# Recurrence stage of a fused attention and mixture-of-experts kernel: two DVE scan operands move from SBUF to PSUM, and the loop's idle matrix products are taken out

## The chip, the cores and the metric

The kernel runs on one core of a Trainium2 chip. The metric is device microseconds (us) of one execution, as the median of several runs. The engines are named as the profile names them: PE multiplies matrices (PEld is its weight load), DVE, ACT and POOL are the vector, scalar and GpSimd engines, SP issues most DMAs. SBUF is the on-chip memory that all of them read; PSUM is the smaller memory into which PE writes its products, in banks of 2 KB per partition (512 f32).

## The reference, cut to what matters

```python
def _attn_ref(r, k, v, w, u):           # B, H, S, D = 2, 8, 768, 48
    state = zeros((B, H, D, D))
    for t in range(S):
        cur = einsum('bhd,bhe->bhde', u * k[t], v[t])
        y[:, :, t] = einsum('bhd,bhde->bhe', r[t], state + cur)
        state = w[t][..., None] * state + einsum('bhd,bhe->bhde', k[t], v[t])
    return y
x = y.transpose(0, 2, 1, 3).reshape(1536, 384)
x = _moe_ref(x)      # one of 8 experts per token: relu(x @ w1[e]) @ w2[e], times its gate weight
return (silu(x @ w_gate) * (x @ w_val)) @ w_out
```

## The kernel before

**Stages.** The recurrence is worked in 12 units of 128 tokens, six for each batch entry (about the first 80 us). A routing tail (to about 97 us) places every token's row in its expert's slots. Then come the eight experts (psh, pso) and the last layer (psg, psu), in which PE has one product behind the other. All work is written out in program order; each engine takes its own instructions in that order, and semaphores hold it where it needs another's result.

**A unit of the recurrence.** Decays are made into running products inside a unit of 2 x 64 tokens. For a unit u, DVE does this, in order:

- `prep1` (L369): two scans X, one for each half, over the decays `dm` (SBUF) with a constant operand `xinit` (SBUF), which is tiny but for a 1 at the place where a head's run starts.
- `xrow` (L533): x = y + aV for the unit before; y is in PSUM, aV in SBUF.
- `state` (L516, L519): d, the decay over a whole unit (4 elements, both operands in SBUF), then Sc = psP * d, the state carried on. PE's product psP stands in the same function, ahead of d.
- `anchored` (L377): the reciprocal of every eighth X into `anch`, in SBUF, one of two buffers.
- `prep2` (L415, L421, L424, L434): two scans R over `wm` (SBUF) and `anch` (SBUF), then M (two multiplies) and rk.

In the loop over u, DVE makes X, R and M for unit u + 2 while PE forms `scores` (psA, from M) for unit u + 1 and `values` (y) for unit u. ACT copies psA out of PSUM, and POOL masks the copy (`affine_select`, L472, reads and writes SBUF) and then makes aV for the next x (`own`, L449, reads SBUF).

**Order of PE in an iteration.** psP of `state(u)`, three idle products (`warm`, psW, 512 columns each, results unused), scores(u + 1), transposes for kgt, the rows psx, the transposes of x, values(u), and one small product `columns` into the tile lg, which holds the gate's logits and a column group a8 that ACT copies out for `own`.

**The names in the prediction.** X, x, d, Sc, R, M, rk, aV, psA, psP, psW, psx, y and lg are tiles as above; `wm` is made by ACT (`prep0`). PSUM tiles with one tag of a pool share a buffer in turn. The lines are those of the kernel before:

Of the kernel before, what the change touches and what calls it, by code (L numbers as in the profile page):

```python
# [24 lines left out]
C = 128  # L25
# [4 lines left out]
G = 8  # L30
# [12 lines left out]
def build(tc, cap, dm, tk, vt, ub, cst, wg, w1, w2, wgate, wval, wout, out):  # L43
# [237 lines left out]
    at = ExitStack()  # L281
    gp = at.enter_context(tc.tile_pool(name="gp", bufs=2))
    ac = at.enter_context(tc.tile_pool(name="ac", bufs=1))
    xinit = ac.tile([128, 2, NP, XW], F32, name="xinit")
    csb = ac.tile([128, 3 * E], F32, name="csb")
    ev, ebase, eend = (csb[:, E * i:E * i + E] for i in range(3))
    ud = ac.tile([128, NP, 32], F32, name="ud")
    fold = ac.tile([128, 32], F32, name="fold")
    wgs = ac.tile([128, 3, 32], F32, name="wgs")
    tri = ac.tile([128, 128], BF16, name="tri")  # L290
    ones = ac.tile([128, 128], BF16, name="ones")
# [6 lines left out]
    early = ExitStack()  # L298
    ep = early.enter_context(tc.tile_pool(name="ep", bufs=2, side="right"))
    dmt = [ep.tile([128, DMW], F32, name=f"dm{i}", bufs=1) for i in range(3)]  # L300
    anch = [ep.tile([128, 2 * (NP * HC + G - 1)], F32, name=f"anch{i}", bufs=1) for i in range(2)]
    wm = [ep.tile([128, 2, NP, HC], F32, name=f"wm{i}", bufs=1) for i in range(2)]
    Sb = [ac.tile([128, NP, 2 * D], F32, name=f"Sb{i}") for i in range(2)]
    ap2 = at.enter_context(tc.tile_pool(name="ap2", bufs=2))
# [1 line left out]
    psA = at.enter_context(tc.tile_pool(name="psA", bufs=1, space=PSUM))  # L306
    ps1 = at.enter_context(tc.tile_pool(name="ps1", bufs=1, space=PSUM))
    psY = at.enter_context(tc.tile_pool(name="psY", bufs=2, space=PSUM))

    vts, Xf, Xt, Mt, kgt, Sc, At, yt, xt, xgt, xgs, av, rkt, a8s, lgt = ({} for _ in range(15))  # L310

    def run(x, up):

        x = x.rearrange("p a b -> p (a b)")
        return x if up else x[:, ::-1]

    def anchors(x, h, o):

        return x[:, h, :, h * o:h * o + HC - G + 1:G]

    def halved(x, w):
        return x[:, 0:2 * NP * w].rearrange("p (h a j) -> p h a j", h=2, a=NP)
# [37 lines left out]
    def prep1(u):  # L360


        if u >= NU:
            return
        W = dmt[u % 3][:, 0:2 * NP * XW].rearrange("p (h a j) -> p h a j", h=2, a=NP)
        Xf[u] = ap3.tile([128, 2 * (NP * XW + G + 1)], F32, tag="X", name="X")
        X = Xt[u] = halved(Xf[u], XW)
        for h in range(2):
            nc.vector.tensor_tensor_scan(out=run(X[:, h], h), data0=run(W[:, h], h), data1=run(xinit[:, h], h),  # L369
                                         initial=0.0, op0=ALU.mult, op1=ALU.max)  # L370
            tick()

    def anchored(u):

        if u >= NU:
            return
        nc.vector.reciprocal(out=each8(anch[u % 2], HC), in_=each8(Xf[u], XW))  # L377
        tick()

    def check(u):  # L380

        if u >= NU:
            return
        for i, t in enumerate((each8(Xf[u], XW), each8(anch[u % 2], HC))):
# [24 lines left out]
    def prep2(u):  # L409

        if u >= NU:
            return
        Rt = ep.tile([128, 2, NP, HC], F32, tag="R", name="R")
        for h in range(2):
            nc.vector.tensor_tensor_scan(out=run(Rt[:, h], 1 - h), data0=run(wm[u % 2][:, h], 1 - h),  # L415
                                         data1=run(halved(anch[u % 2], HC)[:, h], 1 - h),
                                         initial=0.0, op0=ALU.mult, op1=ALU.add)
            tick()
        M = Mt[u] = ap3.tile([128, NP, 4, HC], F32, tag="M", name="M")
        kr = dmt[u % 3][:, 2 * NP * XW:].rearrange("p (a s j) -> p a s j", a=NP, s=4)  # L420
# [32 lines left out]
    def warm(n, ps=None, tag="T"):  # L453

        ps = (ps or psA).tile([128, 512], F32, tag=tag if ps else "A0", name="psW")
        x = xinit.rearrange("p h a j -> p (h a j)").bitcast(BF16)[:, 0:512]
        for _ in range(n):
            nc.tensor.matmul(ps, ones, x, start=True, stop=True)

    def scores(u):  # L460
        if u >= NU:
# [22 lines left out]
    def values(u, ps=range(NP)):  # L484

        if not ps[0]:
            yt[u] = psY.tile([128, DM], F32, tag="y", name="y")
        y, A = yt[u], At[u]
# [12 lines left out]

    def state(u):

        if not (u + 1) % UPB:
            return
        P = ps1.tile([128, NP, D], F32, tag="P", name="psP")
        k = kgt.pop(u)
        if u % UPB:
            nc.tensor.matmul(P, ident, Sc[u], start=True, stop=False, skip_group_check=True)
        for p in range(NP):  # L510
            for g in range(2):
                c0 = D * (2 * p + g)
# [16 lines left out]
    def xrow(u):  # L529
        if u < 0:  # L530
            return
        x = xt[u] = gp.tile([128, DM], F32, tag="x", name="x", bufs=7)
        nc.vector.tensor_tensor(out=x, in0=yt.pop(u), in1=av.pop(u), op=ALU.add)  # L533
        tick()

    gss = {}
# [64 lines left out]
    def choose(us, weigh=weigh):  # L601

        n = len(us)
        u0, u1 = us[0], us[-1] + 1
        lg = lgt[us][:, :, 0:E]

        def over(x):
            return x.to_broadcast([128, n, E])
# [38 lines left out]
    def count(us):  # L647

        u0, n = us[0] // 4 * 4, len(us)
        pc = lgt[us][:, :, 2 * E:]  # L650
        adds = [(ohacc, us[0])] * (u0 > 0) + [(ohs[:, q, :], max(us[0], q + 1)) for q in range(u0, us[-1])]
        nc.tensor.matmul(pc, tri, ohs[:, us[0]:us[-1] + 1, :], start=True, stop=False, skip_group_check=True)
# [204 lines left out]
    nc.vector.memset(xinit[:, 0, :, HC:HC + 1], 1.0)  # L857
    nc.vector.memset(xinit[:, 1, :, 1:2], 1.0)
    for i in range(2):
        nc.gpsimd.memset(wm[i], 0.0)  # L860
        nc.vector.memset(anch[i], 0.0)
    nc.vector.memset(ones, 1.0)
    prep0(0)
    prep1(0)
    anchored(0)
# [22 lines left out]
    for u in range(NU - 2):  # L888
        chosen, counted = ended.get(u - 2), ended.get(u - 3)
        if u:  # L890
            prep0(u + 2)
            prep1(u + 2)
        xrow(u - 1)
        state(u)
        anchored(u + 2)
        warm((7, 4)[u] if u < 2 else 3, ps1, "xT")
        scores(u + 1)
        if u:
            own(u)
# [3 lines left out]
        else:  # L903
# [6 lines left out]
            warm(2, ps1, "lg")  # L910
        expand(u)
        load_dm(u + 4)
        zero(NZ)
# [3 lines left out]
            ready += counted  # L917
        prep2(u + 2)
        if not u:
            check(1)  # L920
            nc.vector.tensor_copy(out=tri, in_=before)
        check(u + 2)
        if u:
            values(u)
            columns(u - 1, max(u - 2, 0), u + 1)
        else:
            values(u)
            for q in range(2):
                to = logits_to(q)
                nc.tensor.matmul(to[:, 0:E], gss.pop(q), fold[:, E:2 * E], start=True, stop=True)  # L930
            a8 = gp.tile([128, 2, H], F32, tag="a82", name="a82")
            nc.scalar.copy(out=a8, in_=lgt[group[0]][:, 0:2, 0:E])
            for q in range(2):
                a8s[q] = a8[:, q, :]
            own(0)
# [625 lines left out]
```

## Time and profile before

| | us |
|---|---|
| median of 3 runs | 465.55 (465.39 to 465.67) |
| the profiled execution, its own time | 465.57 |
| span of its trace, first to last instruction | 463.9 |
| recurrence loop, first X to the last rk | 3.76 to about 79.6 |
| experts' first product | 97.14 |

The profiled execution agrees with the median to 0.02 us; 1.67 us of its own time lie outside its span. A row of a timeline gives start and length in us, engine, line, operation, output <- inputs, shape and count, and in brackets what the engine sat idle for. [...]

### The profile page before, as it was taken

To read this page: it belongs to the slowest core of one execution; us is meant where nothing else is said; L and a number is where in the kernel's file an instruction comes from. 1 tells how busy PE (TensorE), PEld (TensorE's weight loads), DVE (VectorE), ACT (ScalarE), POOL (GpSimd) and SP (SyncE) were. 2 spreads that over 40 slices of the span, in tenths; PEclk is the share of its full clock that TensorE was granted. 3 is DMA by queue.
4 is the path that set the end of the run, shared out by engine and by line. 5 is a ranking of instruction groups with operands and counts; after the bars stand their busy time and mean duration, and the time that the engine had idled before them with its cause. 6 is when DMAs were issued, how large, how long until landed. Compare 5 with 4: busy or idle time off the path is not lost.

```text
span 463.9 us, 9305 instructions
## 1 busy us (share of the span) xinstructions
PE 450.2 (97%) x3565; PEld 397.8 (86%) x3576; DVE 331.0 (71%) x690; ACT 238.8 (51%) x561; POOL 70.9 (15%) x94
## 2 busy tenths in 40 slices
PE   7998999999999999999999999999999999999994
PEld 3676767889999999999988888888888888888884
DVE  8999999877887945858599876665678585434241
ACT  4556685666877866674446454544443352231120
POOL 3324355540000000000000650000000000003033
PEclk9999999999999999999999999999999999999999
DMA  7798994139999944336134455222200000001011
GB/s 247 219 290 266 314 279 163 70 103 305 378 350 361 357 171 144 91 116 199 42 101 131 75 68 70 68 68 69 68 1 0 3 0 0 1 0 69 0 70 68
DMA packets 34801, 62.57 MB, mean 135 GB/s; under 512 B 5504, under 2 KB 17280, under 8 KB 34752
## 3 DMA queue, kind: packets, MB, share of 16 engines
q1 hardware_dynamic: 32832, 57.20, 40.5%
q0 software_dynamic: 1920, 4.73, 2.8%
q8 instruction: 29, 0.48, 0.5%
q14 instruction: 20, 0.16, 0.1%
HBM read 52.48 MB, written 9.44 MB: 133 GB/s over the span
## 4 chain that ended last, share of the span: by engine, by line
PE 80%; DVE 9%; issue 4%; DMA 4%; ACT 1%; POOL 1%; POOLq 0%; SPq 0%; DVEq 0%; ACTq 0%
PE psg L1418 32%; PE psu L1441 14%; PE psh L1297 14%; PE pso L1315 13%; DMA dm<-in_dm 2%; DVE R L415 2%; DVE X L369 2%; DVE M L424 1%; POOL out L1453 1%; PE psA L469 1%; PE y L494 1%; PE y L499 1%; PE psx L1282 1%; DVE rk L434 1%; DVE anch L377 1%
## 5 line engine op out<-in xcount | busy, mean ns | idle before, releaser
L1418 PE MATMUL psg<-yb,wu 128*128 128x512 f32 x648 | 156.3, 395 | 0.0
L1418 PEld LDWEIGHTS psg<-yb,wu 128*128 128x128 f32 x648 | 121.3, 188 | 26.2
L1441 PE MATMUL psu<-wu,a 128*128 128x384 f32 x432 | 80.8, 336 | 0.0
L1441 PEld LDWEIGHTS psu<-wu,a 128*128 128x128 f32 x432 | 76.4, 188 | 2.9
L1297 PE MATMUL psh<-xe,wu 128*128 128x240 f32 x576 | 69.1, 277 | 0.9 <-DVE xe L835 0.9
L1297 PEld LDWEIGHTS psh<-xe,wu 128*128 128x128 f32 x576 | 66.2, 190 | 1.2 <-DVE xe L835 1.1
L1315 PE MATMUL pso<-h,wu 128*128 128x240 f32 x576 | 66.4, 275 | 0.0
L1315 PEld LDWEIGHTS pso<-h,wu 128*128 128x128 f32 x576 | 65.4, 189 | 0.0
L1425 DVE TENSOR_TENSOR t<-t,psg 128x512 f32<-128x512 f32 x36 | 24.7, 686 | 51.9 <-PE psg L1418 38.9
L213 DVE TENSOR_TENSOR wu<-raw,wu 128x512 fp32r<-128x512 f32 x96 | 61.6, 684 | 0.0
L207 ACT CAST wu<-raw 128x512 fp32r<-128x512 f32 x96 | 54.9, 620 | 3.0 <-PE pso L1315 1.4
L1430 ACT CAST a<-t 128x512 fp32r<-128x512 f32 x36 | 22.3, 620 | 60.3 <-DVE t L1425 60.3
L1304 DVE SCALAR_TENSOR_TENSOR h<-psh,h 128x240 fp32r<-128x240 f32 x64 | 25.0, 403 | 23.2 <-ACT h L1303 22.9
L207 ACT CAST wu<-bits 128x384 fp32r<-128x384 f32 x36 | 18.0, 513 | 42.0 <-DVE bits L200 41.9
L1453 POOL DMA_INDIRECT out<-acc,idc x12 | 11.7, 975 | 173.6 <-DVE acc L1451 172.1
L1330 POOL DMA_INDIRECT idl<-ids,dests x12 | 13.5, 1124 | 159.0 <-DVE dests L795 155.6
L1424 ACT ACTIVATE t<-psg 128x512 f32<-128x512 f32 x36 | 21.5, 597 | 30.2 <-PE psg L1418 30.1
L1431 DVE TENSOR_TENSOR a<-t,a 128x512 fp32r<-128x512 f32 x36 | 24.8, 689 | 13.2 <-ACT a L1430 13.2
L1303 ACT ACTIVATE h<-psh 128x240 fp32r<-128x240 f32 x64 | 23.3, 374 | 9.8 <-PE psh L1297 9.1
L1451 DVE TENSOR_TENSOR acc<-psu,acc 128x384 f32<-128x384 f32 x24 | 12.9, 558 | 19.9 <-PE psu L1441 19.9
L471 ACT COPY A<-psA 128x512 f32<-128x512 f32 x24 | 12.8, 586 | 19.0 <-PE psA L469 19.0
L472 POOL TENSOR_SCALAR_AFFINE_SELECT A<-A 128x512 f32<-128x512 f32 x24 | 15.4, 665 | 43.6 <-ACT A L471 43.6
(156 smaller groups left out, 554.5 us busy)
## 6 DMA issues: line engine op xcount, KB each, us to landing
raw<-in_moe_w SPq DMA_DIRECT2D x32, 768.0 KB, 10.8
scr<-zrow SPq DMA_DIRECT2D x12, 384.0 KB, 4.9
raw<-in_moe_w_gate SPq DMA_DIRECT2D x6, 768.0 KB, 4.8
raw<-in_moe_w_val SPq DMA_DIRECT2D x6, 768.0 KB, 4.4
raw<-in_moe_w_out SPq DMA_DIRECT2D x6, 768.0 KB, 4.3
dm<-in_dm SPq DMA_DIRECT2D x18, 192.0 KB, 4.4
v<-in_tk SPq DMA_DIRECT2D x12, 192.0 KB, 6.5
dm<-in_dm SPq DMA_DIRECT2D x18, 99.0 KB, 4.7
```

Of the source, the lines that this page charges most:

```text
L207: nc.scalar.copy(out=slot_t[u % NSLOT][:, 0, c:c + n], in_=bits[i])
L213: nc.vector.tensor_tensor(out=w[:, 1, c:c + n], in0=bits.pop(i), in1=R(w[:, 0, c:c + n]), op=ALU.subtract)
L1297: nc.tensor.matmul(ps, w[:, a, k, c0:c0 + 128], xet[e][:, b, k, :], start=n == 0, stop=n == 8)
L1303: nc.scalar.activation(out=h[:, 0, :], in_=ps, func=AF.Relu)
L1304: nc.vector.scalar_tensor_tensor(out=h[:, 1, :], in0=ps, scalar=0.0, in1=R(h[:, 0, :]), op0=ALU.max, op1=ALU.subtract)
L1315: nc.tensor.matmul(ypt[e, d], w[:, a, f % 4, 128 * d:128 * d + 128], h[:, b, :], start=f == 0 and n == 0, stop=f == 7 and n == 2)
L1418: nc.tensor.matmul(gps[i][g], w[:, a, g, k, c0:c0 + 128], yb[t, k][:, c], start=a_ == k == 0, stop=a_ == k == 2)
L1424: nc.scalar.activation(out=t, in_=pg[0], func=AF.Silu)
L1425: nc.vector.tensor_tensor(out=t, in0=t, in1=pg[1], op=ALU.mult)
L1430: nc.scalar.copy(out=a[:, 0], in_=t)
L1431: nc.vector.tensor_tensor(out=a[:, 1], in0=t, in1=R(a[:, 0]), op=ALU.subtract)
L1441: nc.tensor.matmul(out_ps[t, j], att[i][:, c, 128 * j:128 * j + 128], w[:, a, f % 4, :], start=f % FP == 0 and n == 0, stop=f % FP == FP - ...
```

## The change

- `anch` becomes one tile in PSUM (a whole bank, 512 f32), no longer two in SBUF. The reciprocal writes to it and the R scans and ACT's check read from it.
- `xinit` becomes one half's worth (264 f32) in PSUM. It lies in one bank, `tots`, with the state's product psP.
- Since PE writes to that bank and DVE's X scans read from it, `state(u)` (now only the product) is issued before `prep1(u + 2)`, and d and Sc move into `moved(u)` at the place where they stood.
- The small product `columns` goes into columns 384 on of the y tile (made 512 wide), and ACT copies both logits and a8 from there to an SBUF tile `lgs`. `choose` then reads the logits from SBUF for the first eight units.
- `warm` in the loop stays only in its first two turns (7 and 4 products); the eight iterations behind them, which had three each, have none. Its operands are now a tile `idle` of ones.
- ACT's `check(1)` is issued earlier, behind `prep2(1)`.

```diff
-    xinit = ac.tile([128, 2, NP, XW], F32, name="xinit")
-    anch = [ep.tile([128, 2 * (NP * HC + G - 1)], F32, name=f"anch{i}", bufs=1) for i in range(2)]
+    anch = ps1.tile([128, 2 * NP * HC], F32, tag="lg", name="anch")
+    tots = ps1.tile([128, NP * D + NP * XW], F32, tag="P", name="tots")
+    xinit = tots[:, NP * D:]
+    inv = anch.rearrange("p (h a j g) -> p h a j g", h=2, a=NP, g=G)[..., 0]
+    lgs = ac.tile([128, NU - 3, 2 * E], F32, name="lgs")
...
-            nc.vector.tensor_tensor_scan(out=run(X[:, h], h), data0=run(W[:, h], h), data1=run(xinit[:, h], h),
+            nc.vector.tensor_tensor_scan(out=run(X[:, h], h), data0=run(W[:, h], h), data1=xinit,
...
-        nc.vector.reciprocal(out=each8(anch[u % 2], HC), in_=each8(Xf[u], XW))
+        nc.vector.reciprocal(out=inv, in_=each8(Xf[u], XW))
...
-                                         data1=run(halved(anch[u % 2], HC)[:, h], 1 - h),
+                                         data1=turned(anch[:, h * (NP * HC - G + 1):][:, 0:NP * HC], 1 - h),
...
-        P = ps1.tile([128, NP, D], F32, tag="P", name="psP")
+        P = psp[u] = tots[:, 0:NP * D].rearrange("p (a d) -> p a d", a=NP)
...
+    def moved(u):
+
+        if u not in psp:
+            return
+        P = psp.pop(u)
         d = ap2.tile([128, NP], F32, tag="d", name="d")
...
         if u:
             prep0(u + 2)
+            state(u)
             prep1(u + 2)
         xrow(u - 1)
-        state(u)
+        moved(u)
         anchored(u + 2)
-        warm((7, 4)[u] if u < 2 else 3, ps1, "xT")
+        if u < 2:
+            warm((7, 4)[u], ps1, "xT")
         scores(u + 1)
```

On DVE, the order within an iteration stays as it was; what differs is what the scans read and what they wait for. The iteration in which DVE prepares unit 4, before (X_484 is its X, dm1 its decays, anch0 its anchors; the waits name the engine or DMA queue whose semaphore is awaited):

```order
L369 SCALAR_TENSOR_TENSOR X_484<-dm1_111,xinit_94 128x264 [waits DMAHW1_49,DMAHW0_49]
L369 SCALAR_TENSOR_TENSOR X_484<-dm1_111,xinit_94 128x264
L533 TENSOR_TENSOR x_487<-y_452,aV_413 128x384 [waits PE_49,Pool_49]
L516 TENSOR_TENSOR d_499<-X_256,X_373 128x4
L519 TENSOR_TENSOR Sc_501<-psP_489,d_499 128x192 [waits DVE_49,PE_49]
L377 RECIPROCAL anch0_113<-X_484 128x2x32
L415 SCALAR_TENSOR_TENSOR R_553<-wm0_115,anch0_113 128x256 [waits DVE_49,Activation_49]
L415 SCALAR_TENSOR_TENSOR R_553<-wm0_115,anch0_113 128x256 [waits Activation_49]
```

The same iteration in the changed kernel:

```order
L372 SCALAR_TENSOR_TENSOR X_487<-dm1_110,tots_132 128x264 [waits DMAHW1_49,DMAHW0_49,PE_49]
L372 SCALAR_TENSOR_TENSOR X_487<-dm1_110,tots_132 128x264
L543 TENSOR_TENSOR x_490<-y_447,aV_408 128x384 [waits Activation_49,Pool_49]
L526 TENSOR_TENSOR d_492<-X_266,X_378 128x4
L529 TENSOR_TENSOR Sc_494<-tots_132,d_492 128x192 [waits DVE_49]
L380 RECIPROCAL anch_131<-X_487 128x64
L418 SCALAR_TENSOR_TENSOR R_542<-wm0_112,anch_131 128x256 [waits DVE_49,Activation_49]
L418 SCALAR_TENSOR_TENSOR R_542<-wm0_112,anch_131 128x256 [waits Activation_49]
```

The wait for PE has moved from Sc up to the first X scan, and X and R now have one operand in PSUM (tots, anch); d still has both in SBUF.

On PE, the place between one unit's values and the next one's scores, before (psW is the idle product, psA the scores):

```order
L576 MATMUL lg_362<-fold_97,xT_543 128x16 [waits Activation_49]
L509 MATMUL psP_602<-Sc_501,ident_70 128x192 [waits DVE_49]
L513 MATMUL psP_602<-v_369,kgt_530 64x48 [waits DMAHW6_49]
L513 MATMUL psP_602<-v_369,kgt_530 64x48 x7
L458 LDWEIGHTS ones_100
L458 MATMUL psW_617<-xinit_94,ones_100 128x512 [waits PE_49]
L458 LDWEIGHTS ones_100
L458 MATMUL psW_617<-xinit_94,ones_100 128x512
L458 LDWEIGHTS ones_100
L458 MATMUL psW_617<-xinit_94,ones_100 128x512
L469 MATMUL psA_622<-M_556 128x128 [waits DVE_49]
```

The same place in the changed kernel:

```order
L588 MATMUL y_554<-fold_96,xT_532 128x16 [waits Activation_49]
L511 MATMUL tots_132<-Sc_494,ident_70 128x192 [waits DVE_49]
L515 MATMUL tots_132<-v_365,kgt_519 64x48 [waits DMAHW6_49]
L515 MATMUL tots_132<-v_365,kgt_519 64x48 x7
L471 MATMUL psA_605<-M_545 128x128 [waits DVE_49,PE_49]
```

The three idle products are gone, so the scores follow the state's product at once; the state's product keeps its place on PE.

## Rows read from the trace of the kernel before

**Rows 1.** Busy time by stretch: PE, PEld, DVE, ACT, POOL, then granted clock, DMA share, GB/s

```profile
79.40:86.70 7.30, 7.23 (x136) 6.37 (x138) 6.16 (x26) 4.99 (x13) 2.64 (x4) 1.00 0.01 2
20.00:60.00 40.00, 37.40 (x614) 28.68 (x620) 39.07 (x81) 26.00 (x76) 13.78 (x18) 1.00 0.95 293
60.00:80.00 20.00, 19.56 (x336) 15.32 (x338) 19.38 (x37) 13.13 (x45) 12.93 (x15) 1.00 0.75 231
```

**Rows 2.** Chain that ended last: start, length, engine, tile, line

```profile
61.40 0.48 DVE x L533
61.92 0.55 PE psx L547 x3
...
97.14 8.54 PE psh L1297 x72
```

**Rows 3.** DVE groups, 8 to 61.9 us (units 1 to 8): count, busy, mean ns

```profile
L415 DVE TENSOR_TENSOR_SCAN R<-wm,anch 128x256 f32<-128x256 f32 x16 | 14.2, 921 | 0.7
```

**Rows 4.** DVE groups, 3 to 8 us (unit 0, before POOL's first mask)

```profile
L415 DVE TENSOR_TENSOR_SCAN R<-wm,anch 128x256 f32<-128x256 f32 x2 | 1.3, 680 | 0.0
```

**Rows 5.** Timeline of all engines, 31 to 46 us: one iteration

```profile
38.31 0.67 PE L513 MATMUL psP<-v,kgt 128*64 128x48 f32 x16
38.52 0.68 DVE L424 TENSOR_TENSOR M<-dm,R 128x512 f32<-128x512 f32 x1
39.73 1.30 DVE L369 TENSOR_TENSOR_SCAN X<-dm,xinit 128x264 f32<-128x264 f32 x2
41.39 0.15 DVE L516 TENSOR_TENSOR d<-X 128x4 f32<-128x4 f32 x1
41.58 1.22 POOL L472 TENSOR_SCALAR_AFFINE_SELECT A<-A 128x512 f32<-128x512 f32 x2 [4.10 <-ACT A L471]
41.65 0.36 DVE L519 TENSOR_TENSOR Sc<-psP,d 128x192 f32<-128x192 f32 x1
42.77 1.20 POOL L449 TENSOR_TENSOR aV<-v,a 128x384 f32<-128x384 f32 x1
45.02 0.68 DVE L424 TENSOR_TENSOR M<-dm,R 128x512 f32<-128x512 f32 x1
45.75 0.49 PE L469 MATMUL psA<-M 64*128 64x128 f32 x4 [0.96 <-DVE M L424]
```

**Rows 6.** The same iteration's two R scans, each by itself, from two narrow timelines

```profile
42.57 0.77 DVE L415 TENSOR_TENSOR_SCAN R<-wm,anch 128x256 f32<-128x256 f32 x1
...
43.26 1.25 DVE L415 TENSOR_TENSOR_SCAN R<-wm,anch 128x256 f32<-128x256 f32 x1
```

**Rows 7.** Timeline of DVE, 16 to 31 us

```profile
19.08 1.31 DVE L434 TENSOR_TENSOR rk<-dm 128x512 f32<-128x512 f32 x1
...
28.53 0.58 DVE L516 TENSOR_TENSOR d<-X 128x4 f32<-128x4 f32 x1
```

**Rows 8.** Timeline of POOL, 17 to 48 us

```profile
18.86 0.98 POOL L449 TENSOR_TENSOR aV<-v,a 128x384 f32<-128x384 f32 x1 [2.02 <-ACT a L932]
...
28.46 1.22 POOL L472 TENSOR_SCALAR_AFFINE_SELECT A<-A 128x512 f32<-128x512 f32 x2 [3.85 <-ACT A L471]
...
47.66 0.64 POOL L472 TENSOR_SCALAR_AFFINE_SELECT A<-A 128x512 f32<-128x512 f32 x1 [3.70 <-ACT A L471]
```

**Rows 9.** Timeline of PE, 60 to 95 us

```profile
66.22 1.16 PE L469 MATMUL psA<-M 64*128 64x128 f32 x16
...
71.42 0.67 PE L513 MATMUL psP<-v,kgt 128*64 128x48 f32 x16
...
72.78 1.16 PE L469 MATMUL psA<-M 64*128 64x128 f32 x16
...
78.98 0.39 PE L458 MATMUL psW<-xinit,ones 128*128 128x512 bf16 x1
...
86.78 0.81 PE L458 MATMUL psW<-xinit,ones 128*128 128x512 bf16 x3
```

**Rows 10.** Costliest groups on the page: busy, mean ns, idle before

```profile
L1425 DVE TENSOR_TENSOR t<-t,psg 128x512 f32<-128x512 f32 x36 | 24.7, 686 | 51.9 <-PE psg L1418 38.9
```

More of the change, by code (lines that the diff above doesn't have):

```diff
@@ L290, in build @@
     tri = ac.tile([128, 128], BF16, name="tri")
-    ones = ac.tile([128, 128], BF16, name="ones")
+    idle = ac.tile([128, 4 * C], BF16, name="idle")
+    ones = idle[:, 0:C]
     slots = ac.tile([128, NU], I32, name="slots")
@@ L315, in run, with turned @@
         return x if up else x[:, ::-1]
-    def anchors(x, h, o):
-        return x[:, h, :, h * o:h * o + HC - G + 1:G]
+    def turned(x, up):
+        return x if up else x[:, ::-1]
     def halved(x, w):
@@ L383, in check @@
             return
-        for i, t in enumerate((each8(Xf[u], XW), each8(anch[u % 2], HC))):
+        for i, t in enumerate((each8(Xf[u], XW), inv)):
             j = gp.tile([128, 2, NP, HC // G], F32, tag="sum", name="sum")
@@ L455, in warm @@
         ps = (ps or psA).tile([128, 512], F32, tag=tag if ps else "A0", name="psW")
-        x = xinit.rearrange("p h a j -> p (h a j)").bitcast(BF16)[:, 0:512]
         for _ in range(n):
-            nc.tensor.matmul(ps, ones, x, start=True, stop=True)
+            nc.tensor.matmul(ps, ones, idle, start=True, stop=True)
     def scores(u):
@@ L486, in values @@
         if not ps[0]:
-            yt[u] = psY.tile([128, DM], F32, tag="y", name="y")
-        y, A = yt[u], At[u]
+            yt[u] = psY.tile([128, 512], F32, tag="y", name="y")
+        y, A = yt[u][:, 0:DM], At[u]
         V = vts[u]
@@ L514, in state @@
                                  start=not u % UPB, stop=True, skip_group_check=True)
+    psp = {}
+    def moved(u):
+        if u not in psp:
+            return
+        P = psp.pop(u)
         d = ap2.tile([128, NP], F32, tag="d", name="d")
@@ L532, in xrow @@
         x = xt[u] = gp.tile([128, DM], F32, tag="x", name="x", bufs=7)
-        nc.vector.tensor_tensor(out=x, in0=yt.pop(u), in1=av.pop(u), op=ALU.add)
+        nc.vector.tensor_tensor(out=x, in0=yt.pop(u)[:, 0:DM], in1=av.pop(u), op=ALU.add)
         tick()
@@ L563, in logits_to @@
         g = group[u]
+        if g[-1] < NU - 4:
+            return yt[max(yt)][:, DM:DM + 2 * E]
         if g not in lgt:
@@ L576, in columns @@
         nc.tensor.matmul(to[:, 0:2 * E], gss.pop(u), fold[:, 0:2 * E], start=True, stop=True)
+        if w < NU - 4:
+            w = w if q == w + 3 else NU - 4
+            nc.scalar.copy(out=lgs[:, w, :], in_=to)
+            a8s[q] = lgs[:, w, E:]
+            return
         a8s[q] = gp.tile([128, H], F32, tag="a8", name="a8")
@@ L604, in choose @@
         u0, u1 = us[0], us[-1] + 1
-        lg = lgt[us][:, :, 0:E]
+        lg = lgs[:, u0:u1, 0:E] if u1 <= NU - 4 else lgt[us][:, :, 0:E]
         def over(x):
@@ L649, in count @@
         u0, n = us[0] // 4 * 4, len(us)
+        if us[-1] < NU - 4:
+            lgt[us] = (psY if us[-1] < NU - 5 else ps1).tile([128, n, 3 * E], F32, tag="y" if us[-1] < NU - 5 else "lg", name="lg")
         pc = lgt[us][:, :, 2 * E:]
@@ L856, in build @@
     nc.vector.memset(xinit, TINY)
-    nc.vector.memset(xinit[:, 0, :, HC:HC + 1], 1.0)
-    nc.vector.memset(xinit[:, 1, :, 1:2], 1.0)
+    nc.vector.memset(xinit.rearrange("p (a j) -> p a j", a=NP)[:, :, 1:2], 1.0)
     for i in range(2):
         nc.gpsimd.memset(wm[i], 0.0)
-        nc.vector.memset(anch[i], 0.0)
-    nc.vector.memset(ones, 1.0)
+    nc.vector.memset(anch, 0.0)
+    nc.vector.memset(idle, 1.0)
     prep0(0)
@@ L881, in build @@
     prep2(1)
+    check(1)
     prep0(2)
+    state(0)
     prep1(2)
@@ L909, in build @@
             gss.update((q, gs[:, C * q:C * q + C]) for q in range(2))
-            warm(2, ps1, "lg")
+            warm(2, psY, "y")
         expand(u)
@@ L919, in build @@
         if not u:
-            check(1)
             nc.vector.tensor_copy(out=tri, in_=before)
         check(u + 2)
+        values(u)
         if u:
-            values(u)
             columns(u - 1, max(u - 2, 0), u + 1)
         else:
-            values(u)
+            to = yt[0][:, DM:DM + 2 * E].rearrange("p (q e) -> p q e", q=2)
             for q in range(2):
-                to = logits_to(q)
-                nc.tensor.matmul(to[:, 0:E], gss.pop(q), fold[:, E:2 * E], start=True, stop=True)
+                nc.tensor.matmul(to[:, q], gss.pop(q), fold[:, E:2 * E], start=True, stop=True)
             a8 = gp.tile([128, 2, H], F32, tag="a82", name="a82")
-            nc.scalar.copy(out=a8, in_=lgt[group[0]][:, 0:2, 0:E])
+            nc.scalar.copy(out=a8, in_=to)
             for q in range(2):
@@ L963, in build @@
     state(u)
+    moved(u)
     values(u, [0])
```

## The prediction

> **What bounds the kernel now.** I read the busy time by stretch first. From 20 to 60 us DVE is busy for 39.07 of 40 us while PE, ACT and POOL have room; from 60 to 80 us PE (19.56 of 20) and DVE (19.38) are both full [rows 1]. The chain of waits puts the change of hands at 61.9 us: up to there it runs on DVE, the last piece being x, and then on PE, from the transposes of that x on; it reaches the first expert product at 97.14 us, and from there PE is the chain [rows 2]. So a microsecond saved on DVE ahead of 61.9 us, or on PE between there and the tail, should move everything behind it by as much.
>
> Next, what fills DVE. The two R scans of unit 0, made before POOL has anything to do, take 0.680 us each [rows 4]. The sixteen of units 1 to 8 take 0.921 us in the mean [rows 3]. They have the same shape and work on other numbers only, so the difference is a wait that the trace books as busy time. One iteration shows with whom: POOL's mask runs from 41.58 to 42.80 and its aV from 42.77 to 43.97 us [rows 5]. R's first scan starts at 42.57 and takes 0.77; the second starts at 43.26 and takes 1.25 us, to 44.51 [rows 6], 0.54 us after aV's end and so nearly all of its own work behind it. Both engines read SBUF, and a DVE instruction with two SBUF operands gives way to a POOL instruction that has begun. It is the second operand that counts: in the same mask, Sc (one operand in PSUM) takes 0.36 us at 41.65 without a stretch [rows 5], while d, four elements with both operands in SBUF, takes 0.15 us ahead of a mask [rows 5] and 0.58 us at 28.53, behind one that began at 28.46 [rows 7, 8]. The product rk is held likewise at 19.08 (1.31 us) by the aV that began at 18.86 [rows 7, 8].
>
> **The change, part by part.** *R reads its anchors from PSUM.* One SBUF operand is left, as in Sc, so the scans should no longer be held: 16 x (0.921 - 0.680) = 3.86 us off DVE's path before 61.9 us. The six scans behind it gain too, but there PE is the chain.
>
> *X reads its constant from PSUM.* X is not held now (0.65 us a scan, 39.73 and its pair [rows 5]), so this gains nothing. What it does is keep X free where POOL's work would slide under it.
>
> *The price of a PSUM operand.* X, the reciprocal and R are five instructions a unit, 45 in units 0 to 8. The nearest rows are two multiplies of 512 elements, M with both operands in SBUF at 0.68 [rows 5] and L1425 with one in PSUM at 0.686 us [rows 10]: 0 to 0.01 us each, 0 to 0.45 us in all. I take 0. [...]
>
> *No idle products.* In the DVE-bound part they fill PE's time while it waits: psA starts at 45.75 us, behind M's end at 45.70, with PE idle for 0.96 us ahead of it although three idle products stand there [rows 5]. They are worth nothing there. Behind 61.9 us, where PE is the chain, two bursts remain: psP ends at 72.09 and psA starts at 72.78 [rows 9], 0.69 us, and one like it ahead of 66.22. That is 1.38 us, if DVE can follow; an iteration of PE without the burst is 72.09 - 66.22 = 5.87 us, and one of DVE without a held scan is 45.70 - 39.20 less 0.67 (R's two rows span 1.94, unheld 1.27), so 5.83. They match, and I take all of it.
>
> *The state's product ahead of X.* X now waits for psP, which Sc needed some 1.9 us later. In the iteration shown psP ends at 38.98 and X starts at 39.73 [rows 5]: 0.75 us of cover. A DVE iteration 0.6 us shorter eats most of it, but psP also comes up to 0.4 us earlier once the burst doesn't hold psA back from M's end. I price the wait at nothing, with 0.3 us an iteration as the bound; behind it in DVE's queue stand x, Sc, R and M, so a wait here would be paid in full.
>
> *What is late next: d.* Where PE waits for M, the mask follows M's end by 47.66 - 45.70 = 1.96 us [rows 5, 8]; d follows it by 41.39 - 39.20 = 2.19. Before, the burst held psA and so the mask back, and d mostly slipped in first. Without it d meets the mask and waits for its first half, to about 2.6 us behind M's end: some 0.3 us in units 4 to 6, one of which pays 0.43 already [rows 7]. If PE lags M by 0.2 us, d wins again and even that 0.43 goes. So +0.5 to -0.4 us; I take 0.
>
> *rk of unit 2* is held by an aV that comes when PE and ACT let it, not DVE; R's gain ahead of it is partly waited away there: +0.25 us. The memsets end before the first decays land, and `check(1)` lies in ACT's free time: nothing.
>
> *The sum*, on the profiled execution's own 465.57 us (the median of the runs, 465.55, is the same): 465.57 - 3.86 - 1.38 + 0.25 = **460.6 us**. With d's bounds, 0.45 for PSUM and 0.3 in four iterations for X, it is 460.2 to 462.7.
>
> **The rivals.** *The wait moves, and half the gain with it.* d is held in every unit (0.43 in units 5 and 6 and 0.3 in the last three, where DVE then binds PE) and X waits a little: about 1.8 us back, 462.4. For it: DVE and PE come out equal, so neither has slack. Chance 0.15.
>
> [...] Chance 0.05.
>
> *The scans are held all the same*, because of their other SBUF operand. DVE stays at 6.5 us an iteration, the bursts never bind, about 465.3. Against it: x and Sc, which pass through masks. Chance 0.08.
>
> *PE's clock falls: slower.* The idle products may be what keeps it up. [...] Against it: from 79.4 to 86.7 us PE runs without an idle product, between those at 78.98 and 86.78 [rows 9], at a granted clock of 1.00 [rows 1], and the wait of 0.96 us in the loop didn't lower it either; the shorter iterations will leave PE less idle. For it: no longer stretch without them is in this trace, and only loop products of 48 to 128 columns would be left. [...] Chance 0.07.
>
> **How the numbers follow.** The forecast has 0.65. A measurement of this kernel tells about 0.2%, 0.93 us, from no change. Forecast, half gain and PSUM price are all faster (0.85, of which I take 0.02 off for unseen mishaps); the held scans are no change (0.08); the clock and the mishaps are slower (0.09). The range that leaves out those two cases runs from 458.9 (d wins throughout, and X and Sc gain small things) to 464.2 (PSUM price and part of the moved wait).
>
> **What would show it.** R at 0.66 to 0.69 us in every unit, X unchanged; M from M in 5.8 to 6.1 us; PE's psA directly behind M's end or psP's; d at 0.4 to 0.6 us in some units; clock 1.00 throughout; first expert product near 92 us. The prediction is wrong if R still stretches over POOL's rows, if X shows idle time ahead of it that ends with psP, or if the granted clock dips between 25 and 80 us.

## The result and the profile after

The changed kernel takes 459.99 us (median of 4 runs, 459.89 to 460.64) against 465.56 for the kernel before (4 runs); the ratio is 0.9883, with a 95% interval of 0.9871 to 0.9895. The forecast was 460.6 (458.9 to 464.2). The profiled execution has a span of 458.2 us. Here and below, three executions that took over 1.5% longer than the fastest of their kernel are left out (734.19 us in e1, 896.27 in e2, 473.83 in e9). Lines move by the change: R is L418 now (L415 before), X L372, d L526, rk L437, psA L471, the mask L474, aV L452; psP is the tile `tots`.

The groups of DVE from 8 to 58 us, units 1 to 8, answer [rows 3]; the columns are count, busy us, mean ns and idle time ahead:

```profile
L372 DVE TENSOR_TENSOR_SCAN X<-dm,tots 128x264 f32<-128x264 f32 x18 | 11.8, 686 | 0.0
L418 DVE TENSOR_TENSOR_SCAN R<-wm,anch 128x256 f32<-128x256 f32 x16 | 10.2, 674 | 0.7
L526 DVE TENSOR_TENSOR d<-X 128x4 f32<-128x4 f32 x7 | 1.1, 151 | 0.0
```

R has lost its whole excess: 0.674 us in units 1 to 8, where it was 0.921, and no more than the unheld 0.680 of unit 0 [rows 3, 4]. X, with one PSUM operand more, is where it was (0.686 against 0.688). The two rows of a pair overlap by some 0.08 us (X's pair spans 1.29 us below, where 2 x 0.686 is 1.37). d, which I expected to be held in some units, stands at 0.15 in all of these.

PE's psA, one for each turn of the loop (a turn is one pass over u; the first row here is that of turn 2), timeline:

```profile
25.25 1.16 PE L471 MATMUL psA<-M 64*128 64x128 f32 x16
31.05 1.16 PE L471 MATMUL psA<-M 64*128 64x128 f32 x16
36.85 1.16 PE L471 MATMUL psA<-M 64*128 64x128 f32 x16
42.35 1.16 PE L471 MATMUL psA<-M 64*128 64x128 f32 x16 [0.97 <-DVE M L427]
47.73 1.16 PE L471 MATMUL psA<-M 64*128 64x128 f32 x16
54.76 1.16 PE L471 MATMUL psA<-M 64*128 64x128 f32 x16 [1.27 <-DVE t L697]
60.89 1.16 PE L471 MATMUL psA<-M 64*128 64x128 f32 x16
66.99 1.16 PE L471 MATMUL psA<-M 64*128 64x128 f32 x16 [0.23 <-DVE M L427]
73.51 1.16 PE L471 MATMUL psA<-M 64*128 64x128 f32 x16
```

Two kinds of turn are to be seen. From 25 to 37 us they take 5.80, and psA waits for nothing: PE, busy for 11.60 of the 11.60 us from 25.25 to 36.85, is the chain. At the end they take 6.13 and 6.10, and the 0.23 ahead of 66.99 is a wait for DVE's M. (The three between, 5.50, 5.38 and 7.03, hold other work: the first batch entry ends there, and routing of the first units is mixed in.) The timeline of DVE and POOL at one turn of each kind shows why:

```profile
25.45 1.29 DVE L372 TENSOR_TENSOR_SCAN X<-dm,tots 128x264 f32<-128x264 f32 x2
...
27.11 0.15 DVE L526 TENSOR_TENSOR d<-X 128x4 f32<-128x4 f32 x1
27.16 1.22 POOL L474 TENSOR_SCALAR_AFFINE_SELECT A<-A 128x512 f32<-128x512 f32 x2 [3.56 <-ACT A L473]
27.29 0.36 DVE L529 TENSOR_TENSOR Sc<-tots,d 128x192 f32<-128x192 f32 x1
...
31.20 1.29 DVE L372 TENSOR_TENSOR_SCAN X<-dm,tots 128x264 f32<-128x264 f32 x2
...
68.86 1.22 POOL L474 TENSOR_SCALAR_AFFINE_SELECT A<-A 128x512 f32<-128x512 f32 x2 [1.18 <-ACT A L473]
69.02 0.50 DVE L526 TENSOR_TENSOR d<-X 128x4 f32<-128x4 f32 x1
```

In the first turn d starts 0.05 us ahead of the mask, in the second 0.16 behind it, and is held for 0.35 us. The experiments show that these 0.35 us hang on a few hundredths. The DMA engines are as full as PE in the first stretch (share 1.01, 0.90 in the like turns before); no experiment varies them, so whether they would bind next is open.

Where the time came from, by three places in the two traces (psA of turn 7, the last psA, the first expert product): before 59.27, 79.30 and 97.14; after 54.76, 73.51 and 91.48. So 4.51 us were won by turn 7, 1.28 behind it, and 0.13 given back in the routing tail. The 5.66 that are left are also what the two profiled executions' own times differ by (465.57 and 459.91); by the medians it is 5.57.

### The profile page after: what moved, and what is told of

It is laid out like the page before. It is cut to its first block, busy times and chain, and to the rows that moved or that the text cites. A ratio compares the mean times of both kernels' runs of the same rounds, so it can differ in the third digit from the quotient of the medians.

```text
span 458.2 us, 9251 instructions
## 1 busy us (share of the span) xinstructions
PE 444.8 (97%) x3552; PEld 396.0 (86%) x3552; DVE 325.3 (71%) x688; ACT 238.4 (52%) x561; POOL 68.3 (15%) x94
## 4 chain that ended last, share of the span: by engine, by line
PE 82%; DMA 6%; DVE 5%; issue 3%; ACT 1%; POOL 1%; POOLq 0%; SPq 0%; DVEq 0%; ACTq 0%
PE psg L1439 32%; PE psu L1462 14%; PE psh L1318 14%; PE pso L1336 13%; DMA dm<-in_dm 5%; PE psA L471 1%; PE y L501 1%; POOL out L1474 1%; DVE X L372 1%; PE y L496 1%; PE psx L1303 1%; DVE M L427 1%; PE psW L460 1%; PE psx L557 1%; DMA scr<-xg,slots 1%
## 5 line engine op out<-in xcount | busy, mean ns | idle before, releaser
L1348 DVE TENSOR_TENSOR yb<-yT,yb 128x512 fp32r<-128x512 f32 x27 | 18.5, 684 | 4.4 <-ACT yb L1347 4.4
L474 POOL TENSOR_SCALAR_AFFINE_SELECT A<-A 128x512 f32<-128x512 f32 x24 | 15.0, 649 | 41.3 <-ACT A L473 41.3
```

## The experiments

Three groups of four kernels, each group on one chip beside the kernel before. In the first and third the kernel before took 469.46 and 469.32 us, in the second 465.66: in every trace of the first and third the granted clock falls below 1.00 somewhere from 80 to 100 us (to 0.66 to 0.98 in the mean of 10 us), in none of the second. What makes the groups differ is open: the record gives the first two the same chip number, 2, and the third 0. Across groups I therefore compare ratios, and in the traces the place of the last psA, which lies ahead of that stretch. The changed kernel itself was run only where the kernel before takes 465.6 us, so that its ratio is the same beside 469.4 is assumed, not shown. The first two rows of the table have R and psA from the first profiles.

| kernel | ratio to before (95%) | R, mean us | last psA, us |
|---|---|---|---|
| before | 1 | 0.921 | 79.30 |
| changed | 0.9883 (0.9871 to 0.9895) | 0.674 | 73.51 |
| e1 before, no idle products | 0.9996 (0.9983 to 1.0009) | 0.865 | 79.44 |
| e2 changed, with idle products | 0.9941 (0.9922 to 0.9960) | 0.674 | 76.62 |
| e3 changed, anchors in SBUF | 0.9997 (0.9983 to 1.0012) | 0.885 | 78.73 |
| e4 changed, X in SBUF, order back | 0.9928 (0.9910 to 0.9946) | 0.674 | 75.18 |
| e5 as e3, without aV | 0.9908 (0.9894 to 0.9923) | 0.757 | 74.19 |
| e6 changed, d ahead of X | 0.9885 (0.9863 to 0.9906) | 0.673 | 73.72 |
| e7 changed again | 0.9884 (0.9869 to 0.9898) | 0.673 | 74.31 |
| e9 changed, no idle products at all ahead of turn 2 | 0.9926 (0.9914 to 0.9939) | 0.674 | 76.16 |
| e10 as e6, idle products in turns 5 and 7 | 0.9894 (0.9878 to 0.9910) | 0.673 | 74.22 |
| e11 changed, idle products in turn 7 | 0.9915 (0.9887 to 0.9943) | 0.674 | 74.18 |
| e12 as e4, d ahead of X | 0.9889 (0.9856 to 0.9922) | 0.674 | 73.02 |
| e13 as e9, d ahead of X | 0.9896 (0.9880 to 0.9913) | 0.673 | 75.29 |

My theory after the result: POOL held R through its second SBUF operand, and the sum of terms in the prediction holds. The rivals: the idle products alone did it; the two edits need each other; something else in the change moved POOL's work away from R.

### The two main edits, one at a time (e1, e2)

```diff
# e1, in the kernel before
-        warm((7, 4)[u] if u < 2 else 3, ps1, "xT")
+        if u < 2:
+            warm((7, 4)[u], ps1, "xT")
# e2, in the changed kernel: the reverse
```

> The kernel before without the three idle products of turns 2 and up, nothing else. If the terms of my sum add, this alone is worth the 1.38 us of its term: 464.2. If the two main edits need each other, it is worth little: R is still held, one iteration of DVE behind 61.9 us takes 6.42 (the second M at 65.37 and 71.79) against 6.56 of PE (psA at 66.22 and 72.78), so PE may gain 0.14 in each of two iterations before DVE stops it: 465.3, R at 0.92 as before. Clock 1.00 by both; the clock rival wants a granted clock below 1.00 between 25 and 80 us.

> The changed kernel with the three idle products of turns 2 and up put back. If the terms add: 460.0 + 1.4 = 461.4. If the edits need each other: PE's iteration between 25 and 42 us is 5.80 without an idle moment (psA at 25.25, 31.05, 36.85), so a burst of 0.70 makes it 6.5 there in three turns, and in the last three it costs 0.70 less some 0.2 of idle time: about 3.6 us in all, 463.6, with R still at 0.67 and DVE idle ahead of X or x.

e1 is worth next to nothing: 469.66 us against 469.46. R is still held (0.865), so psA waits for M in six of the eight turns, and two of the waits are 1.6 us. Behind each of them the granted clock fell to 0.50 (from 48 to 50 and from 62 to 64 us), which I had given to neither theory. Timeline of PE in e1, and the stretches of its first wait (length, then busy time of PE, PEld, DVE, ACT and POOL, then the granted clock, DMA share and GB/s):

```profile
45.57 1.16 PE L469 MATMUL psA<-M 64*128 64x128 f32 x16 [1.59 <-DVE M L424]
...
59.43 1.16 PE L469 MATMUL psA<-M 64*128 64x128 f32 x16 [1.61 <-DVE M L424]
```

```profile
44.00:46.00 2.00, 0.43 (x7) 0.46 (x9) 2.00 (x5) 0.74 (x3) 0.00 (x0) 1.00 1.04 351
46.00:48.00 2.00, 2.00 (x29) 1.51 (x28) 2.00 (x5) 1.27 (x3) 0.55 (x1) 0.74 1.05 377
48.00:50.00 2.00, 2.00 (x25) 1.28 (x19) 1.90 (x3) 0.90 (x3) 1.84 (x3) 0.50 1.03 255
```

PE was busy for 0.43 of the 2 us up to 46, and from 48 to 50 the granted clock is 0.50. At psA of turn 5 e1 is 0.18 us ahead of the kernel before (45.57 against 45.75); by the last psA it is 0.14 behind. So the clock can fall in this loop without its idle products, as my rival on the clock had it: to 0.50 here, in the kernel in which R is held, and to 0.50 in e7, below, in the changed one.

The dips also blur what e1 says. Its runs with the mean granted clock that the kernel before mostly has (0.993 and 0.994) take 468.60 to 468.97 us, but for one of 469.50; the kernel before takes 469.19 to 469.73 at 0.994 and 0.995, and e1's other six runs, at 0.984 to 0.991, take 469.66 to 470.27. Sorted like this, after the fact, e1 is worth some 0.7 us where the clock holds, half of the 1.38, and loses it again where the clock falls.

e2 gives half of the gain: 2.7 us of the loop (last psA 76.62 against 79.30), not the 4.2 that remain if 1.38 is taken from 5.57. R is short, and yet PE's turns of 2 to 4 are as long as before:

```profile
25.94 1.16 PE L471 MATMUL psA<-M 64*128 64x128 f32 x16
32.49 1.16 PE L471 MATMUL psA<-M 64*128 64x128 f32 x16
39.05 1.16 PE L471 MATMUL psA<-M 64*128 64x128 f32 x16
44.18 1.16 PE L471 MATMUL psA<-M 64*128 64x128 f32 x16 [0.21 <-DVE M L427]
```

They take 6.55 and 6.56 us, as in the kernel before, where 5.80 stands in the changed one: a burst of about 0.7 us makes PE the chain as soon as DVE's turn is shorter than 6.5. So in these turns R's 0.5 us a turn is lost in full; it is kept where PE has room (17.30 us from psA of turn 4 to that of turn 7, 19.60 in the kernel before). By ratio, R with the other edits brings 0.6%, the idle products alone 0.0% (0.15% where the clock holds), all together 1.2%. e2's interval has the 463.6 of the second theory in it (0.9958) and not the 461.4 of the first (0.9911): the second theory holds, the edits need each other.

### Who holds R (e3, e5)

```diff
# e3, in the changed kernel (e5 as well)
+    anchs = [ep.tile([128, 2 * NP * HC], F32, name=f"anch{i}", bufs=1) for i in range(2)]
-    anch = ps1.tile([128, 2 * NP * HC], F32, tag="lg", name="anch")
...
-        nc.vector.reciprocal(out=inv, in_=each8(Xf[u], XW))
+        nc.vector.reciprocal(out=invs[u % 2], in_=each8(Xf[u], XW))
# e5: x adds a tile of zeros, and POOL makes no aV in the loop
-            own(u)
+            a8s.pop(u)
+            av[u] = zrow[:, 0:DM]
```

> The changed kernel with the anchors back in two SBUF tiles, as before, and nothing else. If POOL's work holds R because of its second SBUF operand, R goes back to about 0.92 in units 1 to 8, and the time to 460.0 + 16 x 0.247 = 463.9, or up to 465.3 if DVE then binds behind 61.9 us too. If R's gain came from something else in the change (POOL's work moved against R by the earlier mask), R stays at 0.67 to 0.7 and the time at 460.

> The changed kernel with the anchors in SBUF again and without POOL's product aV (x adds a tile of zeros in its place, so that part of the result is left out). If it is aV that holds R, R is back at 0.67 to 0.69 although it reads two SBUF operands, and the time is within 0.5 us of the changed kernel's, or 2 us above it if d meets the mask in every turn. If the second SBUF operand costs by itself, R stays at 0.88.

e3 loses the whole gain (ratio 0.9997), and R stands at 0.885: nothing but the anchors' place, and their second buffer, differs from the changed kernel. It loses 5.2 us of the loop, more than the 3.4 of its scans (16 x (0.885 - 0.674)), as d is held too (0.295 in the mean of seven against 0.151, 1.0 us); some 0.8 I haven't traced.

e5 was to bring R back to 0.68 without aV. It came down to 0.757, a miss in the size. (The output of e5 lacks aV, so only its times mean anything.) Two turns of R show what is left, first both engines at 22 us, then R alone at 28:

```profile
22.08 1.62 POOL L474 TENSOR_SCALAR_AFFINE_SELECT A<-A 128x512 f32<-128x512 f32 x2 [5.24 <-ACT A L473]
22.57 1.66 DVE L418 TENSOR_TENSOR_SCAN R<-wm,anch 128x256 f32<-128x256 f32 x2
28.71 1.29 DVE L418 TENSOR_TENSOR_SCAN R<-wm,anch 128x256 f32<-128x256 f32 x2
```

At 22.57 the pair takes 1.66 us, under a mask; at 28.71, where the mask of 27.66 is all but over, 1.29, with 1.26 as the unheld pair of the changed kernel. In e3, with aV, the pairs of the same turns take 1.86 and 1.53. So aV was the greater part, and the mask holds R as well. The hold goes both ways: the mask at 22.08, beside R, takes 1.62 us where the one at 27.66 takes 1.22, and aV takes 1.20 beside R in the kernel before [rows 5] and 0.83 in the changed one. The ratio of 0.9908 lies between e3 and the changed kernel; part of what is missing is d, held in the last two turns (0.49 each).

### X in PSUM and the order (e4, e12), and d ahead of X (e6, e7)

```diff
# e4
-    xinit = tots[:, NP * D:]
+    xinit = ac.tile([128, NP * XW], F32, name="xinit")
...
             prep0(u + 2)
-            state(u)
             prep1(u + 2)
         xrow(u - 1)
+        state(u)
         moved(u)
# e6 in the changed kernel; e12 the same in e4, where state(u) stands behind xrow: d in a function of its own, ahead of the X scans
             prep0(u + 2)
             state(u)
+            ratio(u)        # d = the last X of unit u times the first of unit u + 1
             prep1(u + 2)
```

> The changed kernel with X's constant in an SBUF tile and the state's product back behind x's issue, as before; R's anchors stay in PSUM. By my steps X was never held and its wait for psP costs nothing: 460.0, within 0.3, X at 0.69. Rival: POOL's work slides under X once R is short, X shows 0.8 to 1.2 in some units, and the time is 461 or more. The other rival: X's wait for psP does cost in the changed kernel, and this one is faster by 0.2 to 1.0.

> The changed kernel once more, as the yardstick for the others of this group. On a chip where the kernel before takes 469.5 us instead of 465.6, because every kernel there has a stall of DVE of 2 us near 86 to 91 us and a granted clock of 0.5 behind it, both theories expect the ratio of 0.988 again, within 0.002; if the gain depends on the clock staying at 1.00, the ratio is nearer 1.

> The changed kernel with d made ahead of the X scans (its operands are there a turn earlier) and nothing else moved. If d meets the mask only where DVE is late (0.50 instead of 0.15 in the last two turns, which take 6.10 and 6.08 instead of 5.75), d is at 0.15 in all units and the time 0.4 to 0.7 us less than the changed kernel's. Rival: PE, whose turn of 5.80 is the same, takes all of it: no difference.

> X's constant in SBUF and the state's product behind x again, but with d ahead of the X scans. If what these two edits did for the changed kernel is only that d gets ahead of the mask, the time is the changed kernel's or a little less: 459.3 to 460.3, and the last psA at about 73.5 us against 75.18 without the move of d. If X in PSUM or the order has a worth of its own, it is 461 or more.

e4 was forecast at no difference and lost 1.67 us at the last psA. Neither of its rivals is the reason: X stands at 0.692 and has no wait. It is d and, once, Sc; timeline of e4:

```profile
19.90 1.29 DVE L372 TENSOR_TENSOR_SCAN X<-dm,xinit 128x264 f32<-128x264 f32 x2
...
21.57 0.15 DVE L526 TENSOR_TENSOR d<-X 128x4 f32<-128x4 f32 x1
21.82 0.36 DVE L529 TENSOR_TENSOR Sc<-tots,d 128x192 f32<-128x192 f32 x1
...
25.72 1.30 DVE L372 TENSOR_TENSOR_SCAN X<-dm,xinit 128x264 f32<-128x264 f32 x2
...
27.26 1.22 POOL L474 TENSOR_SCALAR_AFFINE_SELECT A<-A 128x512 f32<-128x512 f32 x2 [3.56 <-ACT A L473]
27.39 0.52 DVE L526 TENSOR_TENSOR d<-X 128x4 f32<-128x4 f32 x1
28.45 0.36 DVE L529 TENSOR_TENSOR Sc<-tots,d 128x192 f32<-128x192 f32 x1 [0.54 <-PE psx L557]
...
34.02 0.49 DVE L526 TENSOR_TENSOR d<-X 128x4 f32<-128x4 f32 x1
...
40.17 0.49 DVE L526 TENSOR_TENSOR d<-X 128x4 f32<-128x4 f32 x1
```

d is held in turns 2 to 4, about 0.35 each, and Sc once waits 0.54 us for something; the psx that the view names is not among the operands of Sc, so that wait stays unexplained. Together that is 1.6 us, about the loss of 1.67; turn by turn the match is looser (e4 is 1.94 behind at psA of turn 5).

Why is d late here and not in the changed kernel? In the changed kernel d starts 1.66 us behind X's start (27.11 and 25.45) and the mask 1.91 behind psA's (27.16 and 25.25). So d gets through if X starts less than 0.25 us behind psA. The changed kernel's X starts 0.20, 0.15 and 0.12 behind in turns 2 to 4; in e4's turn 2 it is 0.36 (25.72 and 25.36), and in the changed kernel's last turns 0.37 (67.36 and 66.99). What makes X late in e4 is Sc. In e4, where Sc has to wait for psP, as in the kernel before, it starts 0.25 us behind d's start (21.57 and 21.82; 0.26 in [rows 5]); in the changed kernel, where X has that wait, it starts 0.18 behind (27.11 and 27.29), and X starts 0.60 to 0.63 behind rk's start in turns 2 to 4, against 0.60 in e4's turn 2. So a turn of DVE in which d isn't held is 5.82 us in e4 (X at 19.90 and 25.72), longer than PE's 5.80, and 5.74 to 5.77 in the changed kernel (X at 19.71, 25.45, 31.20 and 36.97). Each state keeps itself up. Where PE is behind, d is free, DVE's turn is 5.75, shorter than PE's 5.80, and PE stays behind. Where psA waits for M, X comes one rk later, d is held, DVE's turn is 6.1, and PE goes on waiting. The move of the wait from Sc to X, which I had priced as a possible cost, is worth some 0.08 us a turn and lets the first state last.

e12 takes d out of the race, and the loss of e4 is gone, with X in SBUF and in the old order; PE's timeline in e12:

```profile
25.36 1.16 PE L471 MATMUL psA<-M 64*128 64x128 f32 x16
31.16 1.16 PE L471 MATMUL psA<-M 64*128 64x128 f32 x16
36.95 1.16 PE L471 MATMUL psA<-M 64*128 64x128 f32 x16
...
60.70 1.16 PE L471 MATMUL psA<-M 64*128 64x128 f32 x16
66.50 1.16 PE L471 MATMUL psA<-M 64*128 64x128 f32 x16
73.02 1.16 PE L471 MATMUL psA<-M 64*128 64x128 f32 x16
```

The turns of the loop shown here are 5.80 now, the last one too (psA at 73.02 belongs to the code behind the loop, which has more in its way), and the last psA comes at 73.02, 0.49 ahead of the changed kernel's. So X in PSUM and the order had no worth here but what they did for d. I undid the two together; one alone wasn't tried. (e12's ratio alone wouldn't show it: its interval is wide, and one of its runs took 468.21 us.)

e6, the same move in the changed kernel, has d at 0.15 in every unit and the last full turn at 5.80 (61.40 to 67.20), but its median, 459.86, isn't told apart from e7's 460.28. Its three runs at a mean granted clock of 0.996 or more take 459.22 to 459.64, the five such runs of the changed kernel (e7 and the first four) 459.69 to 460.06, so the 0.4 to 0.7 may be there where the clock holds; sorted after the fact, that isn't shown. The clock is why the traces don't settle it. Timeline of PE and two stretches, e7:

```profile
54.65 2.00 PE L471 MATMUL psA<-M 64*128 64x128 f32 x16 [1.28 <-DVE t L697]
61.99 1.16 PE L471 MATMUL psA<-M 64*128 64x128 f32 x16
```

```profile
54.00:56.00 2.00, 1.35 (x13) 1.38 (x15) 2.00 (x7) 2.00 (x9) 0.00 (x0) 0.69 1.11 233
56.00:58.00 2.00, 2.00 (x19) 1.43 (x19) 1.97 (x6) 1.82 (x5) 0.67 (x2) 0.50 1.04 282
```

This is the same program as the one profiled first, and here psA of turn 7 takes 2.00 us behind the wait, at a granted clock that falls to 0.50; the turn takes 7.34 us instead of 6.13. e6 shows a dip too, but an earlier one: PE waits 0.94 us ahead of `columns` (52.72), the granted clock is 0.80 from 52 to 54 and 0.50 from 54 to 56 us, and psA at 54.71, without a wait ahead of it, takes 2.05. Both then reach the last psA later than the first profile's 73.51, at 74.31 and 73.72.

### The idle products that are left (e9, e13, e10, e11)

```diff
# e9 in the changed kernel, e13 in e6
-    warm(12, ps1)
-    warm(4, ps1, "xT")
-        if u < 2:
-            warm((7, 4)[u], ps1, "xT")
-            warm(2, psY, "y")
# e10 in e6 (u in (5, 7)), e11 in the changed kernel (u == 7)
+        if u in (5, 7):
+            warm(3, ps1, "xT")
```

> The changed kernel without the idle products that it still has ahead of turn 2 (12, 4, 7, 4 and 2 of them). If the loop's own products keep PE's clock up, the granted clock is 1.00 from 20 us on, and the time is the same, or up to 0.7 us more because PE no longer lags in turn 2 and d then meets the mask in every turn (4 x 0.35, of which PE hides some). If the idle products carry the clock, it is below 1.00 in the first 20 us and the time is 1 to 6 us more.

> No idle products ahead of turn 2, with d ahead of the X scans. If those products paid by letting PE lag so that d gets ahead of the mask, turns of 6.1 become 5.8 and five of them give back 1.5 us: 461.0, within 0.4; what stays is the start, where psA takes 2.08 us instead of 1.16 twice and PE is 1.5 us later at 21.15. If the loss was all in the start, the time stays at 462.5.

> d ahead of the X scans, and three idle products put back in the two turns alone in which PE waits (turns 5 and 7: 0.97 and 1.27 us ahead of psA in the changed kernel). If the granted clock of 0.83 at 50 to 60 us (psA of 2.00 us at 54.65) follows that wait, the clock is 1.00 in all stretches up to 80 us, no run is over 460.0, and the median is 459.2, within 0.3: the changed kernel's undisturbed 459.9 less two turns of 6.1 that become 5.8. Rival: the products hold up psA in those turns: 0.3 to 0.6 us more than that; or the dip has another cause and comes all the same in some runs.

> The changed kernel with three idle products put back in turn 7 alone, where PE waits 1.27 us. They lie inside the wait and so cost nothing; if the wait is what lowers the clock in some runs, the runs lie together at 459.7 to 460.1 and none is at 460.6 or above. If the dip has another cause, some of the runs still lie there.

e9 takes 462.31 us, 2.0 more than e7 in the same group. Timeline of its PE:

```profile
8.29 2.08 PE L471 MATMUL psA<-M 64*128 64x128 f32 x16 [8.29 <-DVE M L427]
13.56 2.08 PE L471 MATMUL psA<-M 64*128 64x128 f32 x16 [0.38 <-DVE M L427]
21.15 1.16 PE L471 MATMUL psA<-M 64*128 64x128 f32 x16
26.73 1.16 PE L471 MATMUL psA<-M 64*128 64x128 f32 x16
32.86 1.16 PE L471 MATMUL psA<-M 64*128 64x128 f32 x16 [0.25 <-DVE M L427]
```

Both losses that I named are there, though the granted clock doesn't show the first (1.00 from 0 to 20 us). The first two psA take 2.08 instead of 1.16, and the third comes 1.5 us late; from then on d is held (0.62, 0.50, 0.49) and the turns take 6.1, since X starts 0.29 behind psA in turn 2 (27.02 and 26.73). It isn't that PE no longer lags, as I had it: in turn 1 X even waits for psP and starts 0.11 behind psA (21.26 and 21.15), where the changed kernel's starts 0.05 behind. Turn 2 adds 0.18, and the line of 0.25 is missed by 0.04. e13, which differs by the move of d alone, has turns of 5.80 there (25.85, 31.65, 37.45), and its last psA comes at 75.29 instead of 76.16, although its psA of turn 7 takes 1.79 us behind a wait of 1.28. So with the products ahead of the loop the first two psA take 1.16 us each, and without them 2.08; what else e9 lost, it lost in d's race, and the move of d gives that back.

e10 and e11 put products into the waits. In both traces the clock is 1.00 from 10 to 80 us and psA of turn 7 takes 1.16. But e11's runs scatter from 463.54 to 468.35 instead of lying together, and e10's trace has a turn of 7.38 us (60.32 to 67.70): X starts 1.29 us behind psA, PE waits 0.77 for the x that follows X, and a copy of ACT waits 1.80 for something that the trace doesn't show. Both missed their numbers, in a group where even the kernel before takes 469.3 us; whether the products keep the clock up in every run is open. No version measured here is faster than the changed kernel by more than the intervals.

## Why the prediction was right

- *R reads its anchors from PSUM, 3.86 us.* Shown by the trace (0.674) and by e3: 16 x (0.921 - 0.674) = 3.95. The holder is POOL: aV for the greater part (e5); that the mask is the rest is read from rows, no run leaves it out. Not all of POOL's work held DVE: M, with both operands in SBUF, took its usual 0.68 us at 60.06, beside an indirect DMA of POOL from 59.40 to 60.56.
- *The price of a PSUM operand, nothing.* Right: R 0.674 against 0.680, X 0.686 against 0.688; the reciprocal 0.552 against 0.546. The PSUM price that the range allows for at its upper end (464.2), and that has a chance of 0.05, is shown by no run: R and X, each with one operand in PSUM, took no longer than they had taken unheld with both in SBUF, and the reciprocal, which writes to PSUM, took 0.006 us more.
- *No idle products, 1.38 us behind 61.9 us and "worth nothing" ahead of it.* The stretch gained 1.28 net (psA of turn 7 to the last: 20.03 us before, 18.75 after), with d held twice in it. The sentence on the part ahead of it fails a little for the kernel before (in turns 2 to 4 its psA already waits for nothing, and e1's psA of turn 4 comes 0.47 earlier, 39.20 against 39.67, of which 0.18 is left in turn 5) and altogether for the change: as soon as R is short, the bursts bind PE there too, and without their removal 2.7 of the 5.8 us in the loop is all that is left (e2). The sum came out since both edits were made; as a list of separate gains it was wrong.
- *d, +0.5 to -0.4, taken as 0.* The mechanism was right, with both ends in one trace: d gets ahead in turns 2 to 4 and 7 (the mean in units 1 to 8 falls from 0.208 to 0.151 by the same group, some 0.4 us in all) and is held in the last two (0.35 each).
- *rk of unit 2, +0.25.* It took 1.32 us (1.31 before), and X behind it came 0.74 us earlier, which is 0.99 for the four scans ahead of it (at the mean excess of 0.247) less 0.25: right.
- *The gain by turn 7* was 4.51 where the terms gave 3.86 - 0.25 = 3.61. R's 0.09 and d's 0.4 were just named. Beside them, `ohs` takes 0.18 instead of 0.53 (-0.35), and the view shows 0.2 instead of 0.5 us of idle time ahead of Sc (-0.3); against that `sm` takes 0.76 instead of 0.14 (+0.62). None of the three was in the sum. That leaves about 0.4 that I haven't traced. So the total, 5.66 us in the profile where the terms gave 4.99, came as near as it did partly by luck.
- *X's wait for psP, nothing.* Right in the execution profiled first: X has no idle time ahead of it in units 1 to 8. That the wait's move would shorten DVE's turn at Sc by some 0.08 us wasn't seen.
- *The clock rival.* Not in the execution profiled first (1.00 from 0 to 110 us), but e7 has it in the changed kernel: one dip in turn 7, which took 1.2 us longer there (7.34 against 6.13). No run of the changed kernel shows a fall that would make it slower than before: its eight runs (the first four and e7) lie from 459.69 to 461.15, against medians of 465.56 and 465.66. By the prediction's own signs e7 tells against it: the clock dips between 25 and 80 us, and behind the dip X waits 0.88 us for psP (at 62.11). I had argued that shorter iterations would leave PE less idle; the longest wait ahead of psA grew from 0.96 to 1.27. And it wasn't so that no longer stretch without idle products is in the trace before: from 90.0 us on there is none, at a granted clock of 1.00, though with the experts' products and not the loop's.

## What to carry to other kernels

Two edits on two engines that alternate can be worth little apart and much together: compare the turn of each engine after the edit, not before it, and sum only what the slower of the two saves. Where two engines are even to 1% (5.80 and 5.75 us a turn here), look for short instructions that start within hundredths of a us of the work that holds them, and move them out of the race rather than count on the order; here d, four elements, decided 0.35 us a turn, and in which of two steady states the loop ran. Idle products that look like waste bound PE in one stretch (turns of 6.55 us in e2, 5.80 without them) and paid in another (the first two psA took 1.16 us each with them, 2.08 without, in e9), so take them out one place at a time.

## What the runs showed of the hardware

- An instruction with one SBUF operand was held too. `sm`, a TENSOR_SCALAR of four elements in place, took 0.76 us here (0.65 in e7, 0.14 in the kernel before), to the end of the aV that had begun 0.09 us earlier, while the TENSOR_REDUCE beside it passed through a mask in 0.15. Timeline of the changed kernel:

```profile
50.63 1.22 POOL L474 TENSOR_SCALAR_AFFINE_SELECT A<-A 128x512 f32<-128x512 f32 x2 [4.39 <-ACT A L473]
50.99 0.15 DVE L650 TENSOR_REDUCE sm<-ex 128x4 f32<-128x32 f32 x1
...
51.83 0.83 POOL L452 TENSOR_TENSOR aV<-v,lgs 128x384 f32<-128x384 f32 x1
51.92 0.76 DVE L600 TENSOR_SCALAR sm<-sm 128x4 f32<-128x4 f32 x1
```

- In these traces a wait's length alone doesn't tell whether the clock falls behind it: it fell to 0.50 behind 0.94 us in e6, 1.28 in e7 and 1.59 in e1, but 1.27 in the first profile and 1.59 in e3 (psA at 45.57) left it at 1.00. What decides is open.
- In e9 the two psA of 2.08 us, 1.8 times their usual length and near the 2.00 and 2.05 of e7 and e6 at 0.50, stand where the profile's granted clock says 1.00. e13 has the same two (8.12 and 13.40), also at 1.00. There the length of psA showed what that column didn't.
